# Attention's readers on VectorE beside the loop of an attention and relu-squared kernel: their step and their place in it

## The chip, the cores and the metric

The kernel runs on one core of a Trainium2 chip. The core has five engines that work side by side, each through a queue of its own: TensorE (PE in the profile, its weight loads PEld), VectorE (DVE), ScalarE (ACT), GpSimd (POOL) and SyncE (SP), which here issues the DMA transfers. The metric is the device time of one execution in microseconds (us).

## What is computed

Two stages follow each other: agent attention over 4 batches of 12480 tokens with 128 channels and 49 agents, and a two-layer network with a squared relu over all 49920 tokens.

```python
def _attn_ref(q, k, v, agents):
    scale = 1.0 / np.sqrt(q.shape[-1])
    def sm(a, b):
        s = scale * (a @ b.transpose(0, 2, 1))
        s = s - s.max(-1, keepdims=True)
        e = np.exp(s)
        return e / (e.sum(-1, keepdims=True) + 1e-09)
    a2k = sm(agents, k)          # 49 x 12480 a batch
    agent_v = a2k @ v            # 49 x 128
    q2a = sm(q, agents)          # 12480 x 49
    return q2a @ agent_v

def _moe_ref(x, w_in, w_out):    # 128 x 2048, 2048 x 128
    r = np.maximum(x @ w_in, 0.0)
    return (r * r) @ w_out
```

## The kernel before

**The loop.** A piece is 960 tokens (8 chunks of 120); there are 13 pieces a batch, 52 in all. `agent_v @ w_in` is made once a batch (`w_make`, into `w_hi` and `w_lo`), so that a piece's softmax weights go straight into the first layer. A step of the loop handles 480 tokens and 256 of the 2048 hidden columns; there are 16 steps a piece, 832 in all. Step i does this: `mm1(i)` multiplies on PE into `h` (L377), `relu(i)` copies it to `rg` on ACT (L383). Two steps make a pair; at the end of the odd step the pair is squared on ACT (`square`, L386), DVE rounds it to a high part `gh` (`high`, L390) and subtracts that to get the low part `gl` (`low`, L394). `mm2` (L405) of a step stands five steps later, multiplies `gh` by both parts of w_out and then `gl` by the high part, and adds up in PSUM over eight steps, the 480 tokens of one token tile; then `store` (L410 to L412) writes the tile out.

**The places in PSUM.** Two tiles, `pair0` and `pair1`, take the sums of `mm2` by turns. The one that `mm2` doesn't fill is the free place: every product of attention (`bank()`) goes there, one at a time, and a reader on ACT or DVE has to take it away before the next product or before the next token tile's first `mm2`. The products that have a DVE reader are `q_scores` (read by `q_shift`: L312 and L317), `v_acc` (read by `v_sum`: L251 for a batch's first piece, L253 for the others), two of `k_max`'s and `a_final`'s. `k_scores` (read by `k_copy`, ACT), `q_transpose` (`q_copy`, ACT) and `w_make` (ACT, then DVE) are read by ACT first.

**The order.** Nothing is scheduled by the program's tools: `at(t, f)` writes down each part with a number, the parts are sorted by it, and each engine's queue has its instructions in that order. In step i, `mm1` has i, `relu` i + .1, `mm2` i + .2, `square` i + .55, `high` i + .6, `low` i + .65. The attention parts get their numbers from `chain`. It goes along a list of (engine, part), adds `hop[from][to]` steps between an engine and the next, and moves a part to a later step while its engine is `taken` in that step by another attention part (or by a store), or, for PE, while the step isn't one of `slots`: three of eight steps, two steps apart, have room for a product. A product and its readers are placed together, so that the reader is at most one step behind. All then stand at the step's number + .5.

`plan_tokens(s)` lists what a piece of q needs: scores, shift (maximum and subtraction on DVE), exp (ACT), sum and inverse (DVE), normalising (POOL), the two parts of the weights (ACT, POOL), transposes (PE), copies (ACT) and, over DMA, `p_b`. All pieces of q are planned first. `plan_batch(b)` then puts the next batch into what is left: 13 times `k_scores` with `k_copy` (ACT) and `k_pmax` (DVE, L175), the overall maximum (`k_max`, two small products on PE), 13 pieces of `v_acc` with their parts (`v_hi` on ACT, `v_lo` on DVE at L229, `k_sub` and `k_lo` on POOL, `k_exp` and `k_hi` on ACT), spread evenly over the steps that remain, and at the end `a_final` and `w_make`. The loads of k, q and v (`k_load`, `q_load`, `v_load`) share five buffers and stand six or eight steps ahead of their first use.

Of the kernel before, what the change touches and what calls it, by code (L numbers as in the profile page):

```python
# [25 lines left out]
def agent_attention_relu2_kernel(ctx: ExitStack, tc: tile.TileContext, qT, kT, v, agT, w_in, w_out, outT):  # L26
# [392 lines left out]
    def at(t, f, *args):  # L419
        steps.append((t, len(steps), f, args))  # L420

    hop = {"PE": {"PE": 1, "ACT": 1, "DVE": 1}, "ACT": {"PE": 2, "ACT": 1, "DVE": 0, "POOL": 0, "SP": 0},
           "DVE": {"PE": 2, "ACT": 1, "DVE": 1, "POOL": 1, "SP": 0}, "POOL": {"PE": 3, "ACT": 2, "DVE": 2, "POOL": 1}}
    second = {m + LAG - (m < NJ): m for m in range(NG)}
    ends = {i for i, m in second.items() if m % NJ == NJ - 1}
    slots = {i for i, m in second.items() if m % NJ in (1, 3, 5)}
    taken = {(e, i) for i in ends for e in ("ACT", "DVE")}

    def chain(t, todo):

        first = prev = None
        while todo:
            n = 1
            while todo[0][0] == "PE" and n < len(todo) and todo[n][1] in reads_bank and todo[n][0] != "PE":
                n += 1
            t += hop[prev][todo[0][0]] if prev else 0  # L440
            while True:
                g, p, ts = t, None, []
                for e, *_ in todo[:n]:
                    g += hop[p][e] if p else 0
                    while (e, g) in taken or (e == "PE" and g not in slots):
                        g += 1
                    ts.append(g)
                    p = e
                if todo[0][0] != "PE" or ts[-1] <= ts[0] + 1:
                    break  # L450
                t += 1
            for (e, f, *args), g in zip(todo, ts):
                taken.add((e, g))
                at(g + .5, f, *args)
            first = ts[0] if first is None else first
            prev, t, todo = p, ts[-1], todo[n:]
        return first, t

    reads_bank = (k_copy, k_max, v_sum, a_final, w_make, q_shift, q_copy)
# [1 line left out]
    def plan_tokens(s, base):  # L461
        todo = [("PE", q_scores, s), ("DVE", q_shift, s), ("ACT", q_exp, s), ("DVE", q_inverse, s),
                ("POOL", q_norm, s), ("ACT", q_hi, s), ("POOL", q_lo, s),
                ("PE", q_transpose, s), ("ACT", q_copy, s)]
        first, end = chain(base, todo if s > 1 else todo[2:])
        if s > 1:
            at(first - 6, q_load, s)
        at(end + .9, q_spread, s)
        assert end + 3 < s * NF, (s, end)

    def plan_batch(b, base):

        end = b * NS * NF
        for n in range(NS):
            if b == 1 and n < AHEAD:
                continue
            first, t = chain(base + int(n * 4.6), [("PE", k_scores, b, n), ("ACT", k_copy, n), ("DVE", k_pmax, n)])
            at(max(base, first - 8), k_load, b, n)
            if n == NS - 2:
                chain(t + 1, [("DVE", k_max, 0)])  # L480
        _, t0 = chain(t + 1, [("DVE", k_max, 1), ("PE", k_max, 2), ("DVE", k_max, 3), ("PE", k_max, 4), ("DVE", k_max, 5)])
        free = {}
        d = (end - 37 - t0) / NS
        for n in range(NS):
            t, r = t0 + 1 + int(n * d), free.get(n - 2, 0) + 1
            first, _ = chain(max(t - 2, r), [("ACT", v_hi, n, 0), ("DVE", v_lo, n, 0)])
            _, t2 = chain(max(t - 1, r), [("ACT", v_hi, n, 1), ("DVE", v_lo, n, 1)])
            at(first - 6, v_load, b, n)
            _, t1 = chain(max(t, r - 3), [("POOL", k_sub, n), ("ACT", k_exp, n), ("ACT", k_hi, n), ("POOL", k_lo, n)])
            _, t = chain(max(t1 + 3, t2 + 2), [("PE", v_acc, n), ("DVE", v_sum, n)])  # L490
            free[n] = t - 1
        _, e = chain(t + 1, [("DVE", a_final, 0, b), ("PE", a_final, 1, b), ("DVE", a_final, 2, b)])
        for j in range(0, NJ, 4):
            _, e = chain(e + 2, [("PE", w_make, b, j // 4, j, 4, 0), ("ACT", w_make, b, j // 4, j, 4, 1), ("DVE", w_make, b, j // 4, j, 4, 2)])
        assert e + 2 < end, (e, end)
        return t + 1
# [23 lines left out]
    for n in range(NS):  # L520
        t = Z + 6.3 + 2.07 * n
# [41 lines left out]
    t = t0 + 15.9  # L563
# [28 lines left out]
    t = 0  # L592
    for b in range(1, B):
        t = plan_batch(b, t)

    for i in range(NG + LAG):
        if i < NG:
            at(i, mm1, i)
            at(i + .1, relu, i)
            if i % 2:  # L600
                at(i + .55, square, i // 2)
                at(i + (1.5 if i == 1 else .6), high, i // 2)
                at(i + (1.55 if i == 1 else 1.25 if i + 1 in ends else .65), low, i // 2)
        if i in second:
            at(i + .2, mm2, second[i])
            if i in ends:
                at(i + .2, store, second[i] // NJ)
# [28 lines left out]
```

## Time and profile before

| what | us |
|---|---|
| median of three runs | 1985.52 |
| lowest, highest | 1985.49, 2004.62 |
| the profiled execution's own time | 1983.65 |
| its span, from the first to the last instruction | 1981.8 |
| PE busy with matmuls, of the span | 1951.1 |
| DVE busy | 1744.7 |
| ACT busy | 1727.8 |

The span falls into a set-up of some 75 us, in which weights are converted and batch 0's attention is made, and the loop of 832 steps. Rows of a timeline have the start, the duration, engine, line, operation, output<-input and shapes; in brackets stands how long the engine was idle before, and who ended that. Groups of instructions show their count, busy time, mean ns of one, and idle time before them. Windows have, for each stretch, its length, the busy time of PE, PEld, DVE, ACT and POOL with counts, then the clock that TensorE was granted (1.00 is full), the share of DMA and GB/s.

### The profile page before, as it was taken

What the parts mean: (1) busy time and instruction counts of PE and PEld (TensorE: products, weight loads), DVE (VectorE), ACT (ScalarE), POOL (GpSimd) and SP (SyncE); (2) the same over time, 40 slices, a digit from 0 to 9 for tenths busy, and PEclk for the clock granted to TensorE, in tenths of its full rate; (3) what the DMA queues carried; (4) which work ended last, traced back from release to release, by engine and by line L of the source; (5) the groups of instructions that cost most, each with busy time, mean ns of one, the idle gap of its engine ahead of it and who ended that gap; (6) DMA issues with size and microseconds to landing.
All of it is one profiled execution on the core that took longest, in us unless ns stands there. A gap on an engine that the chain in (4) does not pass through costs nothing.

```text
span 1981.8 us, 45743 instructions
## 1 busy us (share of the span) xinstructions
PE 1951.1 (98%) x20140; PEld 1851.3 (93%) x20140; DVE 1744.7 (88%) x1472; ACT 1727.8 (87%) x1810; POOL 309.0 (16%) x202
## 2 busy tenths in 40 slices
PE   9899999999999999999999999999999999999999
PEld 7699998899899998999989999899998899999998
DVE  7688899999888889999988888999998898888887
ACT  4688898898887888999988889899998999999897
POOL 1100013231000112322100101232210101010100
PEclk9999999999999999999999999999999999999999
DMA  8322222221122122122122222122111111101110
GB/s 332 116 61 64 76 66 61 75 85 39 49 81 83 54 68 66 51 83 66 44 66 84 59 66 72 50 72 81 46 51 34 34 51 34 51 29 51 34 41 21
DMA packets 44759, 131.27 MB, mean 66 GB/s; under 512 B 5032, under 2 KB 18472, under 8 KB 44560
## 3 DMA queue, kind: packets, MB, share of 16 engines
q1 hardware_dynamic: 44560, 128.35, 21.1%
q8 instruction: 158, 2.59, 0.5%
q14 instruction: 41, 0.34, 0.1%
HBM read 83.20 MB, written 25.56 MB: 55 GB/s over the span
## 4 chain that ended last, share of the span: by engine, by line
PE 77%; DVE 10%; ACT 7%; issue 4%; DMA 1%; SPq 0%; DVEq 0%; ACTq 0%
PE pair L405 43%; PE h L377 23%; PE pair L165 6%; DVE gl L394 4%; ACT rg L386 3%; DVE gh L390 3%; ACT rg L383 3%; PE pair L351 2%; PE pair L237 2%; DVE vs L229 1%; DMA raw<-w_out 1%; PE h L165 1%; PE pair L288 1%; PE pair L508 1%; DVE e L317 0%
## 5 line engine op out<-in xcount | busy, mean ns | idle before, releaser
L383 ACT ACTIVATE rg<-h 128x960 f32<-128x960 f32 x832 | 806.7, 975 | 199.6 <-PE h L377 199.1
L394 DVE TENSOR_TENSOR gl<-rg,gh 128x1920 fp32r<-128x1920 f32 x416 | 916.8, 2204 | 19.3 <-DVE gh L390 0.5
L386 ACT ACTIVATE rg<-rg 128x1920 f32<-128x1920 f32 x416 | 757.6, 1821 | 5.9
L405 PE MATMUL pair<-gh,wo_hi 64*128 64x480 f32 x3328 | 705.0, 379 | 6.5 <-DVE acc L251 6.5
L405 PE MATMUL pair<-gh,wo_lo 64*128 64x480 f32 x3328 | 703.5, 378 | 0.0
L390 DVE CAST gh<-rg 128x1920 fp32r<-128x1920 f32 x416 | 514.9, 1238 | 165.8 <-ACT rg L386 160.0
L377 PE MATMUL h<-p_a,w_hi 49*128 49x480 f32 x1664 | 543.7, 387 | 0.6 <-ACT rg L383 0.6
L405 PE MATMUL pair<-gl,wo_hi 64*128 64x480 f32 x3328 | 542.5, 379 | 1.8 <-DVE gl L394 1.8
L377 PE MATMUL h<-p_b,w_hi 49*128 49x480 f32 x1664 | 478.5, 387 | 0.0
L405 PEld LDWEIGHTS pair<-gh,wo_hi 64*128 64x128 f32 x3328 | 396.0, 185 | 22.7 <-DVE acc L251 7.7
L405 PEld LDWEIGHTS pair<-gh,wo_lo 64*128 64x128 f32 x3328 | 398.4, 186 | 14.6
L405 PEld LDWEIGHTS pair<-gl,wo_hi 64*128 64x128 f32 x3328 | 372.3, 184 | 18.3 <-DVE gl L394 3.3
L377 PE MATMUL h<-p_b,w_lo 49*128 49x480 f32 x832 | 315.2, 379 | 0.0
L377 PE MATMUL h<-p_a,w_lo 49*128 49x480 f32 x832 | 314.8, 378 | 0.0
L377 PEld LDWEIGHTS h<-p_a,w_hi 49*128 49x128 f32 x1664 | 299.1, 187 | 15.1 <-issue 4.8
L377 PEld LDWEIGHTS h<-p_b,w_hi 49*128 49x128 f32 x1664 | 274.8, 187 | 5.1
L336 POOL TENSOR_TENSOR e<-e,sm 120x392 f32<-120x392 f32 x52 | 57.7, 1109 | 1151.8 <-DVE sm L333 1055.4
L377 PEld LDWEIGHTS h<-p_a,w_lo 49*128 49x128 f32 x832 | 153.7, 185 | 5.9
L377 PEld LDWEIGHTS h<-p_b,w_lo 49*128 49x128 f32 x832 | 153.9, 185 | 1.2
L207 POOL TENSOR_TENSOR pe<-sk,pe 120x392 fp32r<-120x392 f32 x39 | 77.1, 1978 | 269.3 <-ACT pe L204 220.3
L343 POOL TENSOR_TENSOR pp<-e,pp 120x392 fp32r<-120x392 f32 x52 | 102.2, 1965 | 89.3 <-ACT pp L340 89.3
L165 PEld LDWEIGHTS pair<-ag_sb,qt 64*120 64x120 f32 x1632 | 97.3, 182 | 1.0
(102 smaller groups left out, 1297.5 us busy)
## 6 DMA issues: line engine op xcount, KB each, us to landing
vt<-v SPq DMA_DIRECT2D x52, 520.0 KB
kt<-kT SPq DMA_DIRECT2D x52, 480.0 KB
qt<-qT SPq DMA_DIRECT2D x52, 480.0 KB
outT<-ob SPq DMA_DIRECT2D x104, 240.0 KB
p_b<-p_a SPq DMA_DIRECT2D x104, 183.8 KB
raw<-w_in SPq DMA_DIRECT2D x4, 512.0 KB
raw<-w_out SPq DMA_DIRECT2D x4, 512.0 KB
ag_sb<-agT SPq DMA_DIRECT2D x1, 196.0 KB
```

Source lines behind the costliest of these rows:

```text
L165: nc.tensor.matmul(ps[:CH, u, c * A:(c + 1) * A], x[rg[u], h, c, :], ag_sb[rg[u], b, h, :], start=h == 0, stop=h == 1)
L207: eng.tensor_tensor(out=pes[n][:, :, A:], in0=piece(n), in1=pes[n][:, :, :A].bitcast(F32), op=ALU.subtract)
L237: nc.tensor.matmul(pss["v", n][:A2, u, :VW], pe[rc[u], c, :], vs[rc[u], c], start=c == 0, stop=c == G - 1)
L336: eng.tensor_tensor(out=es[s], in0=es[s], in1=sms.pop(s).to_broadcast([CH, G, A]), op=ALU.mult)
L343: eng.tensor_tensor(out=pps[s][:, :, L:], in0=es.pop(s), in1=pps[s][:, :, :A].bitcast(F32), op=ALU.subtract)
L351: nc.tensor.matmul(pss["t", s][u][:, c, :], pp[rc[u], c, :], ident_r[rc[u], rc[u]], start=True, stop=True)
L377: nc.tensor.matmul(h[:, u, :TT], w[ra[u], j, :], PT[s][u ^ lo][ra[u], cs, :], start=x == 0, stop=x == 2)
L383: nc.scalar.activation(rgs[p][:, x], hs.pop(i)[:, :, :TT], AF.Relu)
L386: nc.scalar.activation(rgs[p], rgs[p], AF.Square)
L390: nc.vector.tensor_copy(ghs[p], rgs[p])
L394: nc.vector.tensor_tensor(out=gls[p], in0=rgs.pop(p), in1=ghs[p].bitcast(F32), op=ALU.subtract)
L405: nc.tensor.matmul(outs[t][u][:, :TT], w[rg[u], 2 * j + e, :], g[rg[u], e, :], start=j == 0 and x == 0, stop=j == NJ - 1 and x == 5)
```

## The change

Three things are changed in the planner, and with them where attention's parts stand.

- `hop["PE"]["DVE"]` is 0 in place of 1: a DVE reader that comes right behind its PE product stands in the product's step. In `chain` such a reader doesn't look whether DVE is taken in that step and doesn't take it for others; its step is noted in `read`.
- Products stand at the step's number + .45, and these readers at + .47. All other parts stay at + .5.
- `low` of a pair whose following step has such a reader is emitted at 1.48 behind its odd step, in the following step and behind the reader, in place of .65.

```diff
--- before.py
+++ after.py
@@ -421,12 +421,13 @@
 
 
 
-    hop = {"PE": {"PE": 1, "ACT": 1, "DVE": 1}, "ACT": {"PE": 2, "ACT": 1, "DVE": 0, "POOL": 0, "SP": 0},
+    hop = {"PE": {"PE": 1, "ACT": 1, "DVE": 0}, "ACT": {"PE": 2, "ACT": 1, "DVE": 0, "POOL": 0, "SP": 0},
            "DVE": {"PE": 2, "ACT": 1, "DVE": 1, "POOL": 1, "SP": 0}, "POOL": {"PE": 3, "ACT": 2, "DVE": 2, "POOL": 1}}
     second = {m + LAG - (m < NJ): m for m in range(NG)}
     ends = {i for i, m in second.items() if m % NJ == NJ - 1}
     slots = {i for i, m in second.items() if m % NJ in (1, 3, 5)}
     taken = {(e, i) for i in ends for e in ("ACT", "DVE")}
+    read = set()
 
     def chain(t, todo):
 
@@ -443,6 +444,8 @@
                 for e, *_ in todo[:n]:
                     g += hop[p][e] if p else 0
                     while (e, g) in taken or (e == "PE" and g not in slots):
+                        if p == "PE" and e == "DVE":
+                            break
                         g += 1
                     ts.append(g)
                     p = e
@@ -450,10 +453,15 @@
                     break
                 t += 1
             for (e, f, *args), g in zip(todo, ts):
-                taken.add((e, g))
-                at(g + .5, f, *args)
+                soon = e == "DVE" and prev == "PE"
+                if soon:
+                    read.add(g)
+                else:
+                    taken.add((e, g))
+                at(g + (.47 if soon else .45 if e == "PE" else .5), f, *args)
+                prev = e
             first = ts[0] if first is None else first
-            prev, t, todo = p, ts[-1], todo[n:]
+            t, todo = ts[-1], todo[n:]
         return first, t
 
     reads_bank = (k_copy, k_max, v_sum, a_final, w_make, q_shift, q_copy)
@@ -600,7 +608,7 @@
             if i % 2:
                 at(i + .55, square, i // 2)
                 at(i + (1.5 if i == 1 else .6), high, i // 2)
-                at(i + (1.55 if i == 1 else 1.25 if i + 1 in ends else .65), low, i // 2)
+                at(i + (1.55 if i == 1 else 1.25 if i + 1 in ends else 1.48 if i + 1 in read else .65), low, i // 2)
         if i in second:
             at(i + .2, mm2, second[i])
             if i in ends:
```

There are 98 such readers: 50 `q_shift`, 39 `v_sum`, six of `k_max` and three of `a_final`. Since a chain is a step shorter and DVE is taken less often, the planner also gives many later parts other steps. In batch 1, `k_scores` stands at steps 7, 16, 18, 24, 26, 32, 34 and so on to 58 (before: 7, 16, 24, 26, 32, 40, 42, 48 and so on to 74), `k_max`'s two products at 64 and 66 (before: 80 and 88), `v_acc` at every eighth step from 74 to 170 (before: 98 to 176, two to fourteen steps apart, such as 104, 112, 114, 128 and 130), `a_final`'s product at 176 and `w_make`'s at 178 and 184 (before: 184, 192 and 200).

The first place is DVE's queue around the first `v_sum` of batch 1 (the reader at L251; `vs` is the low part of v, `gh` and `gl` the parts of a pair, `ob` the stored tile). Before, from the inverse of piece 8 on:

```order
L333 RECIPROCAL sm_3646<-sm_3646 120x8
L229 TENSOR_TENSOR vs_650<-vt_3424,vs_650 120x4x128
L390 CAST gh_3675<-rg_3631 128x1920
L394 TENSOR_TENSOR gl_3677<-rg_3631,gh_3675 128x1920
L229 TENSOR_TENSOR vs_650<-vt_3424,vs_650 120x4x128
L251 COPY acc_97<-pair0_103 98x516
L390 CAST gh_3742<-rg_3686 128x1920
L411 TENSOR_TENSOR ob_3765<-ob_3765,pair1_104 128x480
```

Now:

```order
L229 TENSOR_TENSOR vs_650<-vt_2831,vs_650 120x4x128
L390 CAST gh_3029<-rg_2992 128x1920
L251 COPY acc_97<-pair1_104 98x516
L394 TENSOR_TENSOR gl_3069<-rg_2992,gh_3029 128x1920
L229 TENSOR_TENSOR vs_650<-vt_2831,vs_650 120x4x128
L390 CAST gh_3097<-rg_3038 128x1920
L411 TENSOR_TENSOR ob_3120<-ob_3120,pair0_103 128x480
```

The reader has moved from behind the pair's low part and a `v_lo` to straight behind its high part; between that high part and the store stand the same instructions as before. (Lines are those of the kernel before.)

The second place is DVE's queue around the `q_shift` whose scores stand at step 110 (`mx` and `e`, L312 and L317). Before:

```order
L390 CAST gh_4042<-rg_3998 128x1920
L394 TENSOR_TENSOR gl_4044<-rg_3998,gh_4042 128x1920
L312 TENSOR_REDUCE mx_4104<-pair0_103 120x8
L317 TENSOR_TENSOR e_4106<-pair0_103,mx_4104 120x392
L390 CAST gh_4112<-rg_4053 128x1920
```

Now:

```order
L390 CAST gh_4116<-rg_4074 128x1920
L312 TENSOR_REDUCE mx_4155<-pair0_103 120x8
L317 TENSOR_TENSOR e_4157<-pair0_103,mx_4155 120x392
L394 TENSOR_TENSOR gl_4159<-rg_4074,gh_4116 128x1920
L328 TENSOR_REDUCE sm_4185<-e_4157 120x8
```

Both instructions of the reader stand ahead of the low part now, and the sum over `e` (L328) follows at once behind it.

The third is PE's queue at the end of step 18 (L405 is `mm2`, L377 the next step's `mm1`). Before:

```order
L405 MATMUL pair_104<-gh,wo_hi 128x480 x2
L405 MATMUL pair_104<-gh,wo_lo 128x480 x2
L405 MATMUL pair_104<-gl,wo_hi 128x480 x4
L377 MATMUL h<-p_a,w_hi 128x480
L377 MATMUL h<-p_b,w_hi 128x480 x2
```

Now:

```order
L405 MATMUL pair_104<-gh,wo_hi 128x480 x2
L405 MATMUL pair_104<-gh,wo_lo 128x480 x2
L405 MATMUL pair_104<-gl,wo_hi 128x480 x4
L165 MATMUL pair_103<-ag_sb,kt 120x49 x16
L377 MATMUL h<-p_a,w_hi 128x480
```

A `k_scores` product stands in a slot that was empty before.

## The prediction

> **What bounds the kernel now.** I read the page's first part, then the busy time of the engines in one long window of the loop, then PE's own waits there, then the granted clock in short windows, and last the instruction timeline at two of the waits. First the page: the span, the busy times, and DVE's groups with their mean durations in ns behind the comma.
>
> ```profile
> span 1981.8 us, 45743 instructions
> PE 1951.1 (98%) x20140; PEld 1851.3 (93%) x20140; DVE 1744.7 (88%) x1472; ACT 1727.8 (87%) x1810; POOL 309.0 (16%) x202
> L394 DVE TENSOR_TENSOR gl<-rg,gh 128x1920 fp32r<-128x1920 f32 x416 | 916.8, 2204 | 19.3 <-DVE gh L390 0.5
> L390 DVE CAST gh<-rg 128x1920 fp32r<-128x1920 f32 x416 | 514.9, 1238 | 165.8 <-ACT rg L386 160.0 <-PE pair L405 1.9
> L317 DVE TENSOR_TENSOR e<-pair,mx 120x392 f32<-120x392 f32 x51 | 28.9, 567 | 5.3
> L312 DVE TENSOR_REDUCE mx<-pair 120x8 f32<-120x392 f32 x51 | 28.5, 558 | 1.8 <-PE pair L165 1.8
> L253 DVE TENSOR_TENSOR acc<-pair,acc 98x516 f32<-98x516 f32 x36 | 24.0, 667 | 0.0
> ```
>
> PE is busy for 98% of the span: it is the bound, and the change removes none of its matmuls. What can be won is only the time in which PE stands still or runs at a lower clock. The long window runs from 95 us (behind the set-up) to 1976 us; the waits of PE in nearly the same stretch follow (total us, times, longest).
>
> ```profile
> 95.00:1976.00 1881.00, 1865.22 (x19063) 1783.10 (x19061) 1677.68 (x1368) 1672.92 (x1733) 297.41 (x178) 1.00 0.20 59
> ...
> PE pair L237 <- DVE e L317: 8.3, 12, 1.7
> PE pair L405 <- DVE acc L251: 6.5, 3, 2.4
> PE pair L405 <- DVE gl L394: 0.2, 1, 0.2
> PE pair L351 <- DVE ob L411: 0.2, 1, 0.2
> ```
>
> So PE is idle for 1881.00 - 1865.22 = 15.8 us in the loop, and 8.3 + 6.5 = 14.8 us of it have two causes. Twelve times v_acc's products (L237) wait for q_sub (L317), which still reads the free place; three times, once a batch, the first mm2 of a token tile (L405) waits for v_sum (L251), which still reads the place that mm2 is to fill. Both times PE waits for a DVE reader of an attention product.
>
> The waits cost more than themselves. The next windows have the granted clock in the column behind POOL's.
>
> ```profile
> 306.43:309.85 3.42, 3.42 (x22) 2.81 (x20) 3.42 (x4) 1.45 (x2) 3.42 (x2) 0.50 0.46 105
> 374.70:378.11 3.41, 3.41 (x21) 3.40 (x19) 3.34 (x5) 2.13 (x3) 0.37 (x1) 0.50 0.00 0
> 763.82:767.23 3.41, 2.98 (x16) 2.51 (x18) 3.41 (x4) 1.56 (x1) 0.00 (x0) 0.50 0.16 60
> 1251.93:1255.34 3.41, 3.41 (x20) 2.85 (x18) 3.41 (x4) 0.81 (x1) 0.00 (x0) 0.50 0.19 72
> ```
>
> Four stretches of 3.41 us at half clock lie in the loop, three at the three L251 waits and one behind the longest L317 wait (shown below). Half of 4 x 3.41 us is 6.8 us of lost PE time. The most that the change can win in the loop is therefore 15.8 + 6.8 = 22.6 us, apart from what refilling PE's pipeline behind a wait costs.
>
> **Place one, steps 98 to 101, the first v_sum of batch 1.** L237 is v_acc's product, L390 is high, L394 low, L229 v_lo, L251 the reader.
>
> ```profile
> 298.39 1.23 PE L237 MATMUL pair<-vs,pe 56*98 56x258 f32 x16
> ...
> 299.85 1.80 DVE L390 CAST gh<-rg 128x1920 fp32r<-128x1920 f32 x1
> ...
> 301.76 2.16 DVE L394 TENSOR_TENSOR gl<-rg,gh 128x1920 fp32r<-128x1920 f32 x1
> ...
> 303.84 1.51 DVE L229 TENSOR_TENSOR vs<-vt,vs 120x512 fp32r<-120x512 f32 x1
> 305.27 0.68 DVE L251 COPY acc<-pair 98x516 f32<-98x516 f32 x1
> ...
> 306.00 0.49 PE L405 MATMUL pair<-gh,wo_hi 64*128 64x480 f32 x2 [1.79 <-DVE acc L251]
> ...
> 307.43 1.00 PE L405 MATMUL pair<-gl,wo_hi 64*128 64x480 f32 x4
> ```
>
> The product is done at 299.62, DVE has ended high at 301.65, yet it reads the product only at 305.27, behind a low and a v_lo. PE arrives at 306.00 - 1.79 = 304.21.
>
> **Place two, steps 110 to 113.** L165 is q_scores, L312 and L317 its reader.
>
> ```profile
> 328.47 1.79 PE L165 MATMUL pair<-ag_sb,qt 64*120 64x49 f32 x32
> ...
> 330.53 1.15 DVE L390 CAST gh<-rg 128x1920 fp32r<-128x1920 f32 x1
> ...
> 331.71 2.16 DVE L394 TENSOR_TENSOR gl<-rg,gh 128x1920 fp32r<-128x1920 f32 x1
> ...
> 333.79 0.56 DVE L312 TENSOR_REDUCE mx<-pair 120x8 f32<-120x392 f32 x1
> ...
> 334.45 0.57 DVE L317 TENSOR_TENSOR e<-pair,mx 120x392 f32<-120x392 f32 x1
> ...
> 335.16 1.20 PE L237 MATMUL pair<-vs,pe 64*98 64x258 f32 x16 [0.90 <-DVE e L317]
> ...
> 337.71 0.62 PE L405 MATMUL pair<-gl,wo_hi 64*128 64x480 f32 x4
> ```
>
> Here the product is done at 330.26, before high ends at 331.68, and PE comes for the place at 335.16 - 0.90 = 334.26.
>
> **The change part by part.** It adds and removes no instruction. It moves three things.
>
> *The reader ahead of the low.* At place two the reader would run from 331.68: two instructions with the gap between them take from 333.79 to 335.02, 1.23 us, so the place is free at 332.9, 1.3 us before PE comes. The wait of 0.90 goes. At place one the reader would end at 301.65 + 0.68 = 302.3, 1.9 us before PE at 304.21: the wait of 1.79 goes. Since every reader goes at least one low (2.2 us by its group) earlier, and the longest wait is 2.4 us, of which at place one a v_lo of 1.51 us is a part that is passed as well, I take the whole 14.8 us as gone. The two waits of 0.2 us I leave.
>
> *The half clock.* Each of the four stretches stands at a wait of 1.7 us or more; shorter waits (0.9 at place two) have none. With the waits I take the 6.8 us as gone too. The row of the fourth is this one, and its stretch begins at 374.70:
>
> ```profile
> 373.57 1.20 PE L237 MATMUL pair<-vs,pe 64*98 64x258 f32 x16 [1.72 <-DVE e L317]
> ```
>
> *The low behind the reader.* 98 lows are late by a reader: 50 by q_shift (558 + 567 ns and the gap, 1.2 us), 39 by v_sum (0.67), nine by small ones. DVE also takes its queue in order, so a product that is late would hold the low and all that is behind it. At place two the low would end at 331.71 + 2.16 + 1.23 = 335.1. Its mm2 reads it at 337.71, or 336.8 with the wait of 0.90 gone: 1.7 us are left. At place one it would end at 303.92 + 0.68 = 304.6. Without wait and half clock PE would come to that gl at 304.21 plus what lies between L405's first and its gl matmul at full clock. That is 307.43 - 306.00 = 1.43 us at mostly half clock, and not under half of it, 0.7: at 304.9 or later, 0.3 us or more are left. Low ends in time at both places, and next there is little that is late: gl made PE wait once, 0.2 us. What it could cost is not in the trace: nothing at the lower end; at the upper end, if each of the 39 lows behind v_sum were late by half of the 0.67 us that it is moved, 13 us. By place one's 0.3 us of room I take the lower end, with 1 us for some.
>
> *The chains one step shorter.* A reader in its product's step lets what follows start a step earlier, and it no longer counts as taken, so one more slot in 16 steps serves k_scores. The plan of batch 1 ends its k products at step 58 and not 74, and v_acc stands at every eighth step from 74 to 170, before two to fourteen steps apart from 98 to 176. The number of products is the same, and PE's time for them. ACT's k_copy (L172) and DVE's k_pmax (L175) move with their products:
>
> ```profile
> L175 DVE TENSOR_REDUCE pm<-sk 120x49 f32<-120x392 f32 x39 | 33.9, 870 | 6.1 <-ACT sk L172 6.1
> ...
> L172 ACT COPY sk<-pair 120x392 f32<-120x392 f32 x44 | 21.1, 480 | 9.4 <-DVE pm L178 9.4
> ```
>
> In the densest 16 steps 0.48 us on ACT and 0.87 on DVE are added beside a product of 1.79 us on PE (the L165 row above), more than either. PE stays the bound there. The k_load DMAs on SP move with k_scores, and in the plan each still stands two steps or more behind the last reader of the buffer that it takes (five buffers), so SP doesn't hold the p_b and out transfers behind them. POOL's k_sub, q_norm, k_lo and q_lo keep their order in each chain. Nothing is taken for this part; it is in the range by the third rival.
>
> The sum: 1983.65 us is the profiled execution's own time (span 1981.8). 1983.65 - 14.8 - 6.8 + 1 = 1963.05. The median of the runs before is 1985.52, 1.9 above it, but the two fastest of three executions differ by 0.03 only, so I leave the sum as it is: 1963.
>
> [...] By the trace a wait of 1.7 to 2.4 us already has a half-clock stretch at it. [...]
>
> **The rivals.** The third of them needs a slow low and a quick v_lo beside those of place one:
>
> ```profile
> 291.25 2.79 DVE L394 TENSOR_TENSOR gl<-rg,gh 128x1920 fp32r<-128x1920 f32 x1
> 329.93 0.68 DVE L229 TENSOR_TENSOR vs<-vt,vs 120x512 fp32r<-120x512 f32 x1
> ```
>
> - *DVE stands at the head of its queue and low is late (slower).* The reader is now the next instruction behind high, and if the product isn't done, DVE idles, low is late, and mm2 waits for gl instead. It decides if low loses more than its room: to be 1% slower than the median the 98 places would have to cost 22 + 20 = 42 us, 0.43 us each beyond all room. For it speaks place one with only some 0.3 us of room. Against it: both products end 1.4 to 2 us before DVE is free, and ACT rather than PE ended 160.0 of high's 165.8 us of idle time. If it cost 0.5 us at all 98, 49 us, the time would be 1962 + 49 = 2011.
> - *The half clock stays (within 1%).* The waits go, the stretches don't: 1983.65 - 14.8 + 1 = 1970.
> - *Half of the waits come back in new places (within 1%).* The reader is earlier, but v_acc too stands elsewhere, w_make follows a_final by two steps and not by seven, and the second of k_max's products follows the first by two and not by eight. A DVE that is late by POOL's traffic (low 2.79 in place of 2.16, v_lo 1.51 in place of 0.68) would again hold PE: half of 21.6 us lost, 1974. For it speaks that the twelve L317 waits came from such lateness. Against it, that a reader now starts straight behind high.
> - *The readers run no earlier because DVE waits for ACT (no change).* Excluded at both places: high has ended and the product is there. 1984.
>
> **How the numbers follow.** A measurement of this kernel can tell about 1% from no change; 1% below the median is 1965.7. My forecast, 1963 with all but some 2 us of the waits gone, gets 0.64. The clock that stays gets 0.10, half of the waits coming back 0.16, no change 0.05, the late low 0.05. The forecast and no other case lies under 1965.7, but a forecast that misses by 3 us falls above it, so faster gets 0.62 and within 1% 0.34; slower gets 0.04, since part of the late low would only eat the gain. The range reaches down to the bound, 1983.65 - 22.6 = 1961.1, less some 3 us for the refilling of the pipeline that the idle time doesn't hold, 1958, and up to the half that comes back, 1974.
>
> **What would show it.** PE's waits for L317 and L251 gone from the list, at most a few tenths left; the granted clock 1.00 in every loop window; the idle time of PE between 95 and 1950 us at 1 to 2 us. DVE's idle time before L312 and L253 rises if it waits for products, without harm as long as PE's waits for gl stay under 1 us. The prediction is wrong if PE's list is headed by gl, or by the first mm2 of a tile waiting for v_sum again, or if half-clock stretches stand where no wait is.

## The result, and the profile after

The changed kernel takes 1967.2 us in the median of 22 runs, beside 1985.83 us of the kernel before: a ratio of 0.9922, 95% interval 0.9901 to 0.9943. The forecast was 1963, within 1958 to 1974. Its profiled execution took 1969.24 us with a span of 1967.2, beside 1983.65 and 1981.8. Eight of the 22 executions of either kernel took longer than the other fourteen (1979 to 1986 us beside 1963 to 1969, and 1998 to 2005 with one of 2728 beside 1982 to 1987), so that each median lies near the upper end of its larger group.

First the changed kernel's page: the span, the busy times, and two of the groups that stand in the prediction.

```profile
span 1967.2 us, 45731 instructions
PE 1947.6 (99%) x20140; PEld 1862.3 (95%) x20140; DVE 1755.9 (89%) x1472; ACT 1723.0 (88%) x1810; POOL 356.4 (18%) x202
L394 DVE TENSOR_TENSOR gl<-rg,gh 128x1920 fp32r<-128x1920 f32 x416 | 951.0, 2286 | 14.6 <-DVE gh L390 0.5
L390 DVE CAST gh<-rg 128x1920 fp32r<-128x1920 f32 x416 | 502.6, 1208 | 99.6 <-ACT rg L386 95.4
```

Then the loop in one window (length, busy time of PE, PEld, DVE, ACT and POOL with counts, granted clock, DMA share, GB/s).

```profile
95.00:1950.00 1855.00, 1851.30 (x19002) 1783.51 (x19000) 1681.82 (x1364) 1664.75 (x1731) 344.80 (x178) 1.00 0.20 59
```

These are all of PE's waits in it, from 97 us on (us in total, times, longest).

```profile
PE pair L165 <- DMA kt<-kT: 3.1, 1, 3.1
PE h L377 <- ACT rg L383: 0.6, 1, 0.6
```

PE is idle for 1855.00 - 1851.30 = 3.7 us, before 15.8 us. The fifteen waits for L317 and L251, 14.8 us, are gone. A new one stands in their place: once PE waits 3.1 us for a load of k. It costs more than itself, as the next window shows.

```profile
949.51:959.74 10.23, 9.25 (x62) 8.72 (x64) 3.13 (x3) 3.89 (x4) 0.00 (x0) 0.50 0.01 3
```

This is the only half clock left between 95 and 1950 us, 10.2 us long, 5.1 us of PE's time. So the new wait cost some 8 us in this execution. The instructions show why the load is late.

```profile
943.23 0.44 SPq L159 DMA_DIRECT2D kt<-kT  x1
...
950.49 3.44 PE L165 MATMUL pair<-ag_sb,kt 64*120 64x49 f32 x32 [3.10 <-DMA kt<-kT]
```

The load is issued at 943.23 and PE comes for it at 950.49 - 3.10 = 947.39, 4.2 us later. In the plan the load of batch 3's first piece stands at step 377 and its product at 378: `k_load` is put eight steps ahead of its product, though not ahead of the step at which the batch's planning begins, and the new plan has a slot free right behind that step. Before, the load stood at 386 and the product at 394. All the other k loads of the loop stand seven or eight steps ahead.

The two places of the prediction look like this now. First the first `v_sum` of batch 1, now at steps 74 to 77.

```profile
251.72 0.28 PE L237 MATMUL pair<-vs,pe 64*98 64x258 f32 x1
...
252.25 1.15 DVE L390 CAST gh<-rg 128x1920 fp32r<-128x1920 f32 x1
...
253.32 0.69 DVE L251 COPY acc<-pair 98x516 f32<-98x516 f32 x1
...
253.92 2.15 DVE L394 TENSOR_TENSOR gl<-rg,gh 128x1920 fp32r<-128x1920 f32 x1
...
256.25 0.56 PE L405 MATMUL pair<-gh,wo_hi 64*128 64x480 f32 x2
...
257.13 0.78 PE L405 MATMUL pair<-gl,wo_hi 64*128 64x480 f32 x4
```

The reader follows high at once and ends at 254.01; PE comes for the place at 256.25, 2.2 us later, and for the low, which ends at 256.07, at 257.13, 1.06 us later. Then the `q_shift` of step 110.

```profile
331.44 1.84 PE L165 MATMUL pair<-ag_sb,qt 64*120 64x49 f32 x32
...
331.64 1.15 DVE L390 CAST gh<-rg 128x1920 fp32r<-128x1920 f32 x1
...
333.34 0.57 DVE L312 TENSOR_REDUCE mx<-pair 120x8 f32<-120x392 f32 x1 [0.55 <-PE pair L165]
```

Here high ends at 332.79, the product at 333.28, and DVE stands still for 0.55 us between them. That is the wait of the first rival. It is a frequent one, as DVE's waits in the loop show.

```profile
DVE gh L390 <- ACT rg L386: 93.2, 103, 2.0
DVE mx L312 <- PE pair L165: 27.8, 44, 0.9
```

DVE loses 27.8 us at 44 places, 0.63 us each, and PE loses nothing by it: before, DVE stood idle for 160.0 us at high, waiting for ACT, and now for 95.4 (the page's groups). It waits at another place of its queue.

### The profile page after: what moved, and what is told of

The parts are those of the page before. It is cut to its first block, busy times and chain, and to the rows that moved or that the text cites. A ratio compares the mean times of both kernels' runs of the same rounds, so it can differ in the third digit from the quotient of the medians.

```text
span 1967.2 us, 45731 instructions
## 1 busy us (share of the span) xinstructions
PE 1947.6 (99%) x20140; PEld 1862.3 (95%) x20140; DVE 1755.9 (89%) x1472; ACT 1723.0 (88%) x1810; POOL 356.4 (18%) x202
## 4 chain that ended last, share of the span: by engine, by line
PE 95%; DMA 2%; DVE 2%; ACT 1%; issue 0%; SPq 0%; DVEq 0%
PE pair L405 54%; PE h L377 28%; PE pair L165 8%; PE pair L351 2%; PE pair L237 2%; DMA kt<-kT 1%; DMA raw<-w_out 1%; DVE gl L394 1%; PE h L165 1%; PE pair L288 0%; DVE gh L390 0%; PE pair L243 0%; PE pair L516 0%; DMA vt<-v 0%; ACT rg L386 0%
## 5 line engine op out<-in xcount | busy, mean ns | idle before, releaser
L383 ACT ACTIVATE rg<-h 128x960 f32<-128x960 f32 x832 | 805.2, 975 | 188.6 <-PE h L377 188.4
L394 DVE TENSOR_TENSOR gl<-rg,gh 128x1920 fp32r<-128x1920 f32 x416 | 951.0, 2286 | 14.6 <-DVE gh L390 0.5
L386 ACT ACTIVATE rg<-rg 128x1920 f32<-128x1920 f32 x416 | 756.5, 1819 | 5.8
L405 PE MATMUL pair<-gh,wo_hi 64*128 64x480 f32 x3328 | 717.9, 378 | 0.0
L405 PE MATMUL pair<-gh,wo_lo 64*128 64x480 f32 x3328 | 716.5, 377 | 0.0
L390 DVE CAST gh<-rg 128x1920 fp32r<-128x1920 f32 x416 | 502.6, 1208 | 99.6 <-ACT rg L386 95.4
L405 PE MATMUL pair<-gl,wo_hi 64*128 64x480 f32 x3328 | 552.7, 378 | 1.8 <-DVE gl L394 1.8
L377 PE MATMUL h<-p_a,w_hi 49*128 49x480 f32 x1664 | 530.1, 387 | 0.6 <-ACT rg L383 0.6
L377 PE MATMUL h<-p_b,w_hi 49*128 49x480 f32 x1664 | 490.3, 387 | 0.0
L405 PEld LDWEIGHTS pair<-gh,wo_lo 64*128 64x128 f32 x3328 | 420.3, 186 | 13.2
L405 PEld LDWEIGHTS pair<-gh,wo_hi 64*128 64x128 f32 x3328 | 418.1, 184 | 12.8 <-DVE gh L390 0.3
L405 PEld LDWEIGHTS pair<-gl,wo_hi 64*128 64x128 f32 x3328 | 383.0, 184 | 16.5 <-DVE gl L394 3.0
L377 PE MATMUL h<-p_b,w_lo 49*128 49x480 f32 x832 | 315.2, 379 | 0.0
L377 PE MATMUL h<-p_a,w_lo 49*128 49x480 f32 x832 | 314.7, 378 | 0.0
L377 PEld LDWEIGHTS h<-p_a,w_hi 49*128 49x128 f32 x1664 | 290.8, 187 | 14.0 <-issue 4.8
L377 PEld LDWEIGHTS h<-p_b,w_hi 49*128 49x128 f32 x1664 | 275.4, 187 | 4.6
L336 POOL TENSOR_TENSOR e<-e,sm 120x392 f32<-120x392 f32 x52 | 81.9, 1575 | 1070.6 <-DVE sm L333 1038.9
L377 PEld LDWEIGHTS h<-p_a,w_lo 49*128 49x128 f32 x832 | 153.8, 185 | 5.4
L377 PEld LDWEIGHTS h<-p_b,w_lo 49*128 49x128 f32 x832 | 153.9, 185 | 1.3
L343 POOL TENSOR_TENSOR pp<-e,pp 120x392 fp32r<-120x392 f32 x52 | 86.2, 1657 | 151.7 <-ACT pp L340 151.7
L197 POOL TENSOR_TENSOR sk<-sk,mM 120x392 f32<-120x392 f32 x39 | 110.2, 2826 | 0.0
```

Source lines behind the costliest of these rows:

```text
L197: eng.tensor_tensor(out=piece(n), in0=piece(n), in1=m.rearrange("p (o a) -> p o a", o=1).to_broadcast([CH, G, A]), op=ALU.subtract)
L336: eng.tensor_tensor(out=es[s], in0=es[s], in1=sms.pop(s).to_broadcast([CH, G, A]), op=ALU.mult)
L343: eng.tensor_tensor(out=pps[s][:, :, L:], in0=es.pop(s), in1=pps[s][:, :, :A].bitcast(F32), op=ALU.subtract)
L377: nc.tensor.matmul(h[:, u, :TT], w[ra[u], j, :], PT[s][u ^ lo][ra[u], cs, :], start=x == 0, stop=x == 2)
L383: nc.scalar.activation(rgs[p][:, x], hs.pop(i)[:, :, :TT], AF.Relu)
L386: nc.scalar.activation(rgs[p], rgs[p], AF.Square)
```

## The experiments

Beside the times, which hold the set-up too, the loop's length is compared, from the first to the last `mm1` (L377). The row of its first products in the changed kernel reads as follows; behind the durations (ns, min/median/max) stand the first and the last start in us, and the table has these two of each kernel's row. (The first `mm1` of the kernel before starts at 64.1 us, so its set-up is shorter than the 75 us given for it at the start.)

```profile
L377 PE MATMUL h<-p_a,w_hi x1664: 371/377/766, 67.0 to 1953.5; 49*128 49x480 f32 x185
```

| kernel | median us | ratio to before, 95% interval | loop in the profile, us |
|---|---|---|---|
| before | | | 64.1 to 1968.6: 1904.5 |
| the changed kernel | 1967.2 | 0.9922 (0.9901 to 0.9943) | 67.0 to 1953.5: 1886.5 |
| the same again (changed_again) | 1965.85 | 0.9885 (0.984 to 0.993) | 65.8 to 1948.6: 1882.8 |
| early_load | 1960.8 | 0.9891 (0.9853 to 0.9929) | 65.4 to 1943.6: 1878.2 |
| the same again (early_again) | 1959.95 | 0.9854 (0.9811 to 0.9898) | 65.4 to 1944.1: 1878.7 |
| order_alone | 1963.83 | 0.9891 (0.9864 to 0.9919) | 64.7 to 1947.8: 1883.1 |
| plan_alone | 2003.73 | 1.0098 (1.0063 to 1.0132) | 67.5 to 1988.0: 1920.5 |
| plan_late_exp | 1983.72 | 0.9991 (0.9955 to 1.0027) | 85.7 to 1986.4: 1900.7 |
| order_q | 1977.32 | 0.9961 (0.9948 to 0.9975) | 65.3 to 1964.8: 1899.5 |
| order_v | 1979.32 | 0.9986 (0.9963 to 1.0008) | 64.9 to 1962.6: 1897.7 |
| extra_ahead | 2009.01 | 1.0096 (1.0051 to 1.0141) | 67.1 to 1993.7: 1926.6 |
| extra_behind | 2018.07 (2 runs) | 1.0138 (0.9978 to 1.0298) | 66.3 to 1992.5: 1926.2 |

### Is the late load the whole of the new wait?

In the changed kernel:

```diff
-            at(max(base, first - 8), k_load, b, n)
+            at(first - 8, k_load, b, n)
```

> The changed kernel, with each k load eight steps ahead of its product also where a batch begins (batch 3's first load then stands at step 370 and not at 377, one step ahead of its product). If the late load is the whole of the new wait: PE's wait of 3.1 us for kt at 947 us and the 10.2 us at half clock behind it go, no half clock is left in the loop, and the span of the profile falls from 1967.2 to some 1959 (3.1 + 5.1 us less). If the wait came from a transfer that was slow by chance or by other traffic: a wait for kt of 1 us or more stays somewhere in the loop, or the span stays at 1964 or more.

The wait is gone, and with it the half clock behind 95 us. PE's only wait in the loop is that of 0.6 us for `relu` which the changed kernel has too, and the loop's window reads:

```profile
95.00:1950.00 1855.00, 1854.40 (x19071) 1790.28 (x19068) 1689.20 (x1369) 1669.21 (x1733) 344.83 (x178) 1.00 0.20 59
```

PE is idle for 0.6 us in this window, and the whole loop is 8.3 us shorter than the changed kernel's. It was run again beside the changed kernel on one chip.

> The changed kernel with the early k load once more, beside the changed kernel itself on the same chip, since their intervals against the kernel before overlap. If the late load costs what the profile says: 3 to 8 us less than the changed kernel (0.2 to 0.4%), no wait of PE for kt in the loop.

> The changed kernel itself, to be set beside early_again. If the late load is a fixed part of its plan: PE waits some 3 us for kt at step 378 again, with one stretch of half clock or none behind it, of 3.4 or 10.2 us as it may come.

The medians are 1959.95 and 1965.85 us, 5.9 us apart, and the changed kernel's wait for kt is there again, 3.0 us. The half clock behind it was only 3.4 us this time:

```profile
949.71:953.11 3.40, 3.40 (x24) 3.35 (x23) 0.00 (x0) 1.32 (x3) 0.00 (x0) 0.50 0.02 5
```

So the wait is a fixed part of the changed plan, and what the clock adds varies from run to run: 5.1 us in one execution, 1.7 in another. The intervals of the two ratios overlap (0.9811 to 0.9898 and 0.984 to 0.993); that the early load is the faster rests on the medians and on the profiles together. By its medians it is the fastest kernel of this study.

### Which half of the change carries the gain?

The change both emits the readers ahead of low and plans with shorter chains. Each half was run by itself. The first has the changed kernel's plan, with low where it was:

```diff
-                at(i + (1.55 if i == 1 else 1.25 if i + 1 in ends else 1.48 if i + 1 in read else .65), low, i // 2)
+                at(i + (1.55 if i == 1 else 1.25 if i + 1 in ends else .65), low, i // 2)
```

> The changed kernel's plan (products and readers at its steps), but low where it was, ahead of the reader. If the reader's place ahead of low is what took the waits away: PE's waits for the readers (L317, L251, L253) come back at 8 to 15 us, with at least two half-clock stretches in the loop, and the span is 1975 to 1985. If the new plan alone did it (v_acc four steps behind q_scores instead of two, fewer crowded places): these waits stay under 3 us and the span is at 1960 to 1969.

The second has the plan of before, and takes only each reader's emission from the change. In the kernel before, beside the changed kernel's line for `low` and an empty set `read`:

```diff
             for (e, f, *args), g in zip(todo, ts):
                 taken.add((e, g))
-                at(g + .5, f, *args)
+                soon = e == "DVE" and prev == "PE"
+                if soon:
+                    read.add(ts[0])
+                at(ts[0] + .47 if soon else g + .45 if e == "PE" else g + .5, f, *args)
+                prev = e
             first = ts[0] if first is None else first
-            prev, t, todo = p, ts[-1], todo[n:]
+            t, todo = ts[-1], todo[n:]
```

> The plan of before (every product and every follower at its old step), but each DVE reader emitted right behind its product, ahead of the pair's low. If the reader's place ahead of low carries the gain: PE's waits for L317 and L251 are under 1 us in all, no half clock in the loop, span 1959 to 1963, and no wait for kt, since the k loads stand where they were. If the plan carries it: at least half of the 14.8 us of waits stays, span 1972 or more.

order_alone came out as the order's theory has it: no wait for L317 or L251 is left, no half clock from 95 us on, and the whole gain is there, 0.9891. Its window has PE idle for 1.7 us:

```profile
95.00:1950.00 1855.00, 1853.29 (x19025) 1764.26 (x19023) 1680.27 (x1366) 1672.60 (x1733) 346.92 (x178) 1.00 0.20 59
```

plan_alone fits neither expectation. The waits for L317 and L251 did not come back, as the plan's theory had it, and yet it is 1% slower than before. PE's longest waits in its loop:

```profile
PE h L377 <- ACT rg L383: 13.2, 17, 1.3
PE pair L405 <- DVE gl L394: 4.6, 8, 0.9
PE pair L165 <- DMA kt<-kT: 3.2, 1, 3.2
PE pair L288 <- DVE a L275: 2.4, 3, 0.8
PE pair L405 <- DVE acc L253: 1.8, 6, 0.3
```

And one row of ACT's waits, the largest behind relu's wait for `mm1`:

```profile
ACT e L324 <- DVE e L317: 68.3, 50, 2.4
```

ACT waits 68.3 us for the readers, at every one of the 50 `q_shift`. In the instructions of one of them (L383 is `relu`, L386 `square`, L324 `q_exp`):

```profile
262.56 2.79 DVE L394 TENSOR_TENSOR gl<-rg,gh 128x1920 fp32r<-128x1920 f32 x1
...
265.93 0.57 DVE L317 TENSOR_TENSOR e<-pair,mx 120x392 f32<-120x392 f32 x1
...
266.53 0.53 ACT L324 ACTIVATE e<-e 120x392 f32<-120x392 f32 x1 [2.41 <-DVE e L317]
266.97 1.79 ACT L386 ACTIVATE rg<-rg 128x1920 f32<-128x1920 f32 x1
...
268.67 1.82 ACT L383 ACTIVATE rg<-h 128x960 f32<-128x960 f32 x2
...
269.67 0.48 PE L377 MATMUL h<-p_a,w_hi 49*128 49x480 f32 x1 [1.32 <-ACT rg L383]
```

The plan has drawn `q_exp` a step nearer to the scores. The reader, still behind a low of 2.79 us, isn't done, so ACT stands at `q_exp` for 2.41 us with square and relu behind it; relu empties `h` late, and PE's next `mm1` waits 1.32 us. That was a third theory, and it got a run of its own: plan_alone with `q_exp` and `q_inverse` a step later.

```diff
-                at(g + (.47 if soon else .45 if e == "PE" else .5), f, *args)
+                late = f in (q_exp, q_inverse) and args[0] > 1
+                at(g + late + (.47 if soon else .45 if e == "PE" else .5), f, *args)
```

> The plan_alone kernel (low ahead of the reader, the changed kernel's plan) with q_exp and q_inverse emitted one step later, where they stood against their q_scores before the change. If plan_alone loses because ACT stands at q_exp until the late q_shift is done, with square and relu queued behind it: ACT's 68 us of waits for L317 fall under 10 us, PE's 13.2 us of waits for relu's h buffers under 3 us, and the span falls from 2001.7 to 1980 to 1990. If it loses because DVE as a whole is late: the span stays above 1995.

ACT's waits for L317 are gone altogether, PE's waits for relu fell from 13.2 to 1.4 us, and the loop from 1920.5 to 1900.7 us, the median from 2003.73 to 1983.72. The span was 2000.0 and not 1980 to 1990, but not by the loop: this execution's set-up ran at half clock for 51 us, and its first `mm1` starts at 85.7 us instead of 67.5.

```profile
10.84:62.03 51.19, 51.19 (x465) 45.77 (x465) 26.55 (x51) 16.54 (x30) 1.27 (x1) 0.50 0.63 215
```

So the halves are not alike. The order carries the gain by itself. The plan by itself costs 16.0 us in the loop, and all of that because it needs the readers early: with `q_exp` and `q_inverse` put back it is 3.8 us shorter than before. With the plan alone the waits for L317 and L251 are gone too, in both of these kernels; but others stand in their place, and the time hardly falls. With the order in place the plan is worth 1883.1 - 1878.2 = 4.9 us of loop when its late load is mended, and costs 3.4 us as it is (1886.5); the ratios of the first set can't tell these apart.

### Does each reader's place remove its own waits?

In order_alone, only one of the readers was moved: `soon = f is q_shift and prev == "PE"` in order_q, `soon = f is v_sum and prev == "PE"` in order_v.

> The plan of before, with q_shift alone emitted right behind its product and ahead of low; v_sum and the small readers stay where they were. If each reader's place removes the waits for that reader: PE's 8.3 us for L317 go, its 6.5 us for L251 stay at 4 to 7 us with two or three half-clock stretches behind them, span some 1970. If the waits have one common cause (a DVE that is late as a whole): both shrink by about the same part.

> The plan of before, with v_sum alone emitted right behind its product and ahead of low; q_shift and the small readers stay where they were. If each reader's place removes the waits for that reader: PE's 6.5 us for L251 go, its 8.3 us for L317 stay at 6 to 10 us, span some 1972. If the waits have one common cause: both shrink by about the same part.

PE's longest waits in order_q's loop:

```profile
PE pair L405 <- DVE acc L251: 5.5, 3, 2.0
PE pair L237 <- DVE acc L253: 4.1, 5, 1.2
```

And in order_v's:

```profile
PE pair L237 <- DVE e L317: 12.9, 14, 1.7
```

Each moved reader's own waits are gone, and the other's stay: L251's fell by 1.0 us of 6.5, L317's even rose from 8.3 to 12.9. The spans, 1978.1 and 1975.9 us, are longer than the 1970 and 1972 that were expected. In order_q a wait for L253 appears that the kernel before didn't have. A likely reason is that PE, no longer held at one place, comes earlier to the next; no run isolates it. The gain of the moves together is more than the sum of each alone: 0.9961 and 0.9986 against 0.9891, and in the loop 5.0 and 6.8 us against order_alone's 21.4. (order_alone also moves the nine small readers. order_v's interval includes no change; its gain rests on the profile.) Each of order_q's three waits for L251 again has a stretch at half clock, as its windows show:

```profile
307.46:310.87 3.41, 3.41 (x22) 2.80 (x20) 3.41 (x4) 1.67 (x2) 3.41 (x2) 0.50 0.40 116
761.44:764.84 3.40, 3.21 (x16) 2.75 (x18) 3.40 (x4) 1.72 (x2) 0.00 (x0) 0.50 0.19 72
1249.54:1252.95 3.41, 3.41 (x20) 2.82 (x18) 3.41 (x3) 1.63 (x3) 0.28 (x1) 0.50 0.19 72
```

order_v, with fourteen waits of at most 1.7 us, has no such stretch from 95 us on; its mean granted clock was 0.997, order_q's 0.994.

### How much room do the moved lows have?

In early_load, two DVE reductions of a constant go between each `q_shift` or `v_sum` and its low (extra_ahead), or behind the low (extra_behind):

```diff
+    def extra():
+        for _ in range(2):
+            nc.vector.tensor_reduce(out=spare, in_=win_sb[:CH, :G * A].rearrange("p (c a) -> p c a", a=A), axis=AX.X, op=ALU.max)
...
                 at(g + (.47 if soon else .45 if e == "PE" else .5), f, *args)
+                if soon and f in (q_shift, v_sum):
+                    at(g + .475, extra)
```

with .485 in place of .475 for the twin.

> The changed kernel with the early k load and, between each q_shift or v_sum and its low, two more DVE reductions of a constant (some 1.1 us, 89 times), whose result nobody reads. By the changed kernel's trace the lows that were moved end at least 1.06 us (v_sum) and 1.86 us (q_shift) before PE needs them, so none of these makes PE wait by more than 0.1 us. What the queue as a whole loses, because lows further on have 0.1 to 0.5 us of room at a dozen places, costs 5 to 15 us, here and in its twin (the same reductions behind the low) alike: the two differ by less than 4 us. If the moved low is at its limit, so that the late low decides: this one is slower than its twin by 20 us or more, with PE waiting for gl at tens of places.

> The same two reductions at the same 89 places, but behind the low. If the moved lows have room: within 4 us of its twin, some 1962 to 1972. If the moved low is at its limit: 20 us or more faster than its twin.

The page of extra_ahead has these busy times:

```profile
PE 1957.9 (98%) x20140; PEld 1750.6 (87%) x20140; DVE 1853.4 (92%) x1650; ACT 1725.6 (86%) x1810; POOL 304.2 (15%) x202
```

PE's longest wait in its loop (L399 is `low` here):

```profile
PE pair L410 <- DVE gl L399: 26.5, 32, 2.0
```

And in extra_behind's:

```profile
PE pair L410 <- DVE gl L399: 21.4, 31, 1.1
```

The twins' spans are 2007.4 and 2006.1 us, 1.3 apart, as was expected if the moved lows have room: whether 1.1 us stands ahead of a low or behind it makes hardly a difference to the whole. (The medians, 2009.01 and 2018.07, are the other way round, but the second comes from two runs.) But it isn't true of every moved low. In extra_ahead nine of PE's waits for gl are at a low straight behind the two reductions, six of them behind a v_sum (9.7 us in all, up to 2.0), where none above 0.1 us was expected; in extra_behind PE waits for the same six lows too, 5.6 us in all. Five half-clock stretches lie in extra_ahead's loop from 95 us on, one in extra_behind's; the mean granted clocks were 0.992 and 0.996. The size was wrong as well. Some 97 us more of DVE's work (1853.4 beside early_load's 1756.1) cost 2007.4 - 1957.2 = 50 us against early_load, where 5 to 15 were expected, and PE waits for gl at some 30 places in both. DVE as a whole, at 90% busy in early_load, has little left to give; its load, more than the place of one low, would decide next.

## Why the prediction was right

- **The time: right, 1967.2 within 1958 to 1974.** But the case with the highest chance, more than 1% faster (0.62), did not come: a gain of 0.8% lies just within 1%, which had 0.34. The likeliest value was 4 us too low, and that it wasn't further off is partly luck. The sum began at the profiled execution's own time, 2.2 us below the median of 1985.83. It had nothing for a new wait (the late load, some 6 to 8 us), and nothing for some 4 us that the new plan takes off PE's busy time. The last two partly cancel.
- **PE bounds, and only its waits and half clock can be won: right for the order, too narrow for the plan.** The whole loops of the kernel before, of order_alone and of early_load, in this order:

```profile
64.10:1968.60 1904.50, 1887.44 (x19283) 1799.16 (x19283) 1695.84 (x1388) 1695.00 (x1756) 301.32 (x181) 1.00 0.20 58
64.70:1947.80 1883.10, 1879.87 (x19283) 1784.62 (x19282) 1702.48 (x1388) 1695.48 (x1756) 350.84 (x181) 1.00 0.20 59
65.40:1943.60 1878.20, 1876.07 (x19283) 1805.67 (x19283) 1707.22 (x1388) 1689.80 (x1756) 348.74 (x181) 1.00 0.20 59
```

  order_alone's loop is 21.4 us shorter: PE is idle for 13.8 us less (17.1 and 3.2) and busy for 7.6 us less, of which the four half-clock stretches are 6.8. For the refilling of PE's pipeline the range had some 3 us more; that was the author's estimate, no run shows this term by itself, and less than 1 us is left for it here. early_load's loop is another 4.9 us shorter, and 3.8 of that is PE's busy time, though the products are the same and neither has a half-clock stretch from 95 us on. This comes with the new plan; what in it does this was not tried.
- **14.8 us of waits for L317 and L251 go: right,** all fifteen of them. order_alone shows that the reader's place is enough for it, order_q and order_v that each reader does its own. The new plan alone (plan_alone, plan_late_exp) removes them as well, though not the time.
- **6.8 us of half clock go with them: right for those four stretches.** No stretch is left at a reader's wait, and early_load has none from 95 us on. A new one came with the late load, so two of the signs named in the prediction failed: the clock is not 1.00 in every loop window, and PE's idle time between 95 and 1950 us is 3.7 us and not 1 to 2.
- **1 us for lows that are late: too much.** PE doesn't wait for gl in the loop. The room at the first `v_sum` was put at 0.3 us or more; there are 1.06, though nine other moved lows run out of room when extra_ahead adds 1.1.
- **"Nothing is taken for this part", the shorter chains: the step that was mis-sized.** It was argued that each k load stands two steps or more behind the last reader of its buffer. That holds, and it is the wrong end of the load: how far it stands ahead of its product was not looked at, and one stands a single step ahead. It cost some 8 us in the profiled execution and some 6 in the medians; without it the result would be near 1961. The same part of the change also brought the 4 us named above. The third rival had the mechanism's kind (a wait in a new place, 1974), with other places.
- **The kernel doesn't wait at places one and two any more, but DVE does.** The prediction read from two places, both with a late DVE, that the product is done before DVE is free. In the new order DVE waits for the product at 44 of the loop's 50 `q_shift`. The first rival thus happens in its first half; it costs nothing since DVE waits that much less for ACT.
- **A half-clock stretch at each wait of 1.7 us or more and none at a shorter one: so in the four rows of the kernel before, but the length of a wait doesn't settle it.** The three L251 waits of order_q, 5.5 us in all and up to 2.0, each have a half-clock stretch; order_v's fourteen of up to 1.7 us have none; and the wait for kt, 3.1 and 3.0 us in the two profiled executions of the changed kernel, was followed by 10.2 and 3.4 us.

A stretch need not stand at one long wait either. Here are two windows of extra_behind, each with the one that follows:

```profile
433.06:436.48 3.42, 1.93 (x16) 1.03 (x14) 3.42 (x4) 3.42 (x6) 0.00 (x0) 1.00 0.00 0
436.48:439.89 3.41, 3.41 (x18) 2.86 (x20) 3.38 (x6) 2.19 (x3) 0.00 (x0) 0.50 0.00 0
818.77:822.18 3.41, 2.00 (x16) 1.09 (x14) 3.38 (x3) 3.41 (x6) 0.01 (x1) 1.00 0.00 0
822.18:825.60 3.42, 2.95 (x34) 2.62 (x34) 3.42 (x4) 2.50 (x3) 0.10 (x1) 1.00 0.14 52
```

PE is idle for 1.49 us in the first window, more than the longest wait in its list (1.1 us), so this stretch stands behind more than one wait. In the third window PE is idle for 1.41 us, and no half clock follows. What decides whether a stretch begins, and how long it lasts, was not shown by any run. In the changed kernel's profiled execution it began 2.1 us behind the start of the wait for kt (949.51 and 947.39), while PE still waited.

## What to carry to other kernels

When an in-order engine reads a product that others wait for, its place in that queue can be worth more than its share of busy time: here the same instructions in another order took away 15 us of waits on TensorE and 7 us of half clock behind them. Such an order and a plan that counts on it belong together, for the plan without the order was 1% slower than neither. And when a planner fills steps more tightly, look at both ends of every prefetch: how far it stands behind the last reader of its buffer, and how far ahead of its own use.

## What the runs showed of the hardware

- The half clock at a wait was not in proportion to the wait. The stretches shown from the loops of the kernel before, order_q and changed_again are 3.40 to 3.42 us long, at waits of up to 3.0 us; the changed kernel's wait of 3.1 us brought one of 10.23 us.
- The set-up missed full clock for a long time once: in plan_late_exp's profiled execution TensorE ran at 0.50 from 10.8 to 62.0 us, though PE was busy all that time, and the loop began some 18 us later than in plan_alone's. Why it stayed low there was not tried.
- A better order need not make the instructions quicker: low's mean rose from 2204 to 2286 ns between the kernels and high's fell from 1238 to 1208, POOL's busy time rose from 309.0 to 356.4 us, DVE's from 1744.7 to 1755.9, and the kernel is faster all the same.
